# A linear-attention block with a gated FFN on one core: x's last rows written out whole in DRAM, w1's blocks paired into tiles, and the order of additions and lo parts

## The chip, the cores and the metric

The kernel runs on one core of a Trainium2 chip. The core has the engines TensorE (PE in the profile; its weight loads are the row PEld), VectorE (DVE), ScalarE (ACT), GpSimd (POOL) and SyncE (SP). SP issues all DMA transfers here, and sixteen DMA engines carry them out. Times are microseconds of device time of one execution. The kernel before took a median of 1215.95 us over three runs (1214.75 to 1216.89).

## The reference

With x of 2048 x 576 (S x D), 32 heads of 18, and F = 4608:

```
xn  = layernorm(x)
q, k, v = split(xn @ wqkv)                       # 32 heads of 18
pq, pk  = phi(q), phi(k)                         # t + 1 where t > 0, else exp(t); + 1e-6
kv, z   = sum over s of pk v', sum over s of pk
o   = (pq @ kv) / (pq . z + 1e-6)
s   = o @ wo
g   = silu(gelu(xn @ w1 + b1) @ w2 + b2)         # 576 -> 4608 -> 576
out = x + s * g
```

## The kernel before

Every float32 matrix product is made of three fp32r products: an operand is split into a hi part (a cast by ACT) and a lo part (the value less its hi part, one subtraction), and hi x hi, hi x lo and lo x hi are added in PSUM. So each operand costs a copy on ACT and a subtraction, mostly on DVE.

**Phase 1** (to about 155 us) normalises x in sixteen tiles of 128 rows (`t`), makes k and v and adds up kv and z. On the side it forms operands of w2 and stores them in DRAM.

**Phase 2** (to about 298 us) is a loop over `i` = 1 to 19: PE makes the query of tile `i` (`query`), transposes the normalised query of tile `i - 2` (`ptp`, L560) and multiplies that of tile `i - 4` with the folded kv and wo (`attend`, L569). `normalize(i)` has DVE form the sum `den`, and POOL `pbuf` (L543), which the transpose of the next-but-one iteration reads. `beside(i, k)` (L776) places other work there: with k = 0 ahead of `den`, with k = 2 ahead of `normalize`. This is the preparation of x for the FFN.

**The FFN** treats x as two halves of 1024 rows, and each half as two blocks of 512. Both of its products, x @ w1 ("Up") and h @ w2 (the down products, `pm`), use a scheme of seven products in place of eight on 2 x 2 blocks. So x is needed as seven operands (`h0`, `h1`, `s1`, `s2`, `s4` and parts of them, made by `XSums`), and w1 too. The sums sum1 to sum4 of `XSums` are DVE additions of 1024 columns, in the table `SUMS`; `SPLITS` says when each is split into hi and lo. D is 576 = 4 x 128 + 64. The 64 last rows of a block are handled on their own by `Rest`: `gather` collects them, `whole` adds hi and lo, stores them in DRAM (`rr_dram`) and loads them back shifted, `sums` forms the sums, `split` makes hi and lo of q (k = 0) and e (k = 1) and stores these in `rq_dram`. `load_rest` then fills the last column block of an operand, 128 rows of 512: four times the hi rows (one broadcast load of 32 rows), and then the lo rows over rows 32 to 63 (a second load into the same tile). The table `RESTS` says in which iteration each part runs. Half 1 of x is used first; half 0 is kept in `x_dram` and `rq_dram` and loaded at the change of halves (`load_x_part`, L1183).

The FFN runs 18 steps: nine groups of 512 columns of w1 (and rows of w2) for half 1 of x, called the first half here, and the same nine for the other half, the second half. A step has two Ups (j = 0 and 1, one `W1` object each, n = 2 step + j) and then 14 down products, and so 28 places, numbered 0 to 27 from its base: 7 for each Up, one per product in the order UP = (1, 6, 7, 5, 2, 3, 4), and 14 for the down products. After each, `at_step` emits the work that the plan has put there. DVE, ACT, POOL and PE execute exactly in the order in which this emits (`in_order`, L55); only SP's order is left to the scheduler.

In the first half a `W1` loads two raw blocks of w1 (`w1raw`), POOL forms the sums for products 5, 6, 7 and 4 in place (`T`, L627), and for each tile `hi` copies (ACT), `lo` subtracts (DVE, two instructions: L657 and, for the last rows, L659) and stores the tile in DRAM. `P1` and `P0` give the places of `T`, `hi` and `lo`. Step s takes the `W1` of its second Up through `P1` in places 0 to 4, that is during its first Up, and that of the next step's first Up through `P0`, with "a" (blocks 1 and 2 in one tile) in place 14 and the rest in 24 to 27. In the second half `W1Loaded` loads the stored tiles.

An Up (L912 to L939) has one PSUM tile each for its products; DVE adds them: u1 after product 6 (L921), u2 after 7 (L924), b after 5 (L927, in place of PSUM's B), e after 3 (L934), zy after 4 (L938), and GELU on ACT follows b, e, zy and a (after product 2). Product 3 adds on to the same PSUM bank E that L927 reads, so PE can't begin it before L927 has run. `at_step` comes behind the product's own addition. Of h, POOL forms the sums (L991 to L1000), ACT and DVE the hi and lo parts (`h_h`, `h_l`); `macc` (L1040) is DVE's addition of down products. After the change of halves `start_with_b2` loads b2 into `macc` once more.

Of the kernel before, what the change touches and what calls it, by code (L numbers as in the profile page):

```python
# [8 lines left out]
F32 = mybir.dt.float32  # L9
# [31 lines left out]
def linear_attention_gated_ffn(ctx, tc, x, wqkv, wo, w1, b1, w2, b2, out):  # L41
# [274 lines left out]
    class XSums:  # L316
# [290 lines left out]
    W1_N = {"a": 10, "b": 5, 4: 5, 5: 5, 6: 5, 7: 5}  # L607
    W1_TAG = {"a": ("wa", 2), "b": ("wb", 2)}

    def w1_tile(i, n):  # L610
        tag, bufs = W1_TAG.get(i, ("wt", 5))
        return w1p.tile([P, W1_N[i], P], F32R, tag=tag, name=f"w{i}_{n}", bufs=bufs)

    class W1:
# [3 lines left out]
        def __init__(self, n):  # L618
            self.n = n
            raw = stage_w1(f"w1raw{n}")  # L620
            nc.sync.dma_start(raw, w1[n % NP])
# [24 lines left out]
        def hi(self, i):  # L646
            self.tiles[i] = t = w1_tile(i, self.n)
            nc.scalar.copy(t[:, : 6 if i == "a" else 3], self.src[i])

        def lo(self, i):  # L650
            t, src = self.tiles[i], self.src[i]
            if i == "a":
                two = lambda v: v.rearrange("p (h k) c -> p h k c", h=2)
                hi, src, lo = two(t[:, :6]), two(src), two(t[:, 6:])
            else:
                hi, src, lo = t[:, None, :3], src[:, None], t[:, None, 3:]
            EL1.tensor_tensor(lo, src[:, :, :2], hi[:, :, :2].bitcast(F32), op=SUB)  # L657
            r = hi[64:96, :, 2]
            EL1.tensor_tensor(r, src[64:96, :, 2], r.bitcast(F32), op=SUB)  # L659
            keep_op(w1_dram, (self.n, i), t)  # L660

        def product(self, i):

            if i in (1, 2):
                t, k = self.tiles["a"], i - 1
                return t[:, 3 * k : 3 * k + 2], t[:, 6 + 2 * k : 8 + 2 * k], t[:, 3 * k + 2]
            t = self.tiles["b" if i == 3 else i]
            return t[:, :2], t[:, 3:], t[:, 2]
# [27 lines left out]
    class Rest:  # L696
# [4 lines left out]
        def tmp(self, tag, n):  # L701
            bufs, k = (2, 10) if tag == "wa" else (5, 5)
            t = w1p.tile([P, k, P], F32R, tag=tag, name=f"rest{self.half}{n}", bufs=bufs)
            return t.rearrange("p k c -> p (k c)")

        def gather(self):
            t = self.tmp("wa", "q").bitcast(F32)
            self.q, lo = t[:, :512], t[:, 512:1024]
# [6 lines left out]
        def whole(self):  # L715
# [3 lines left out]
            t = self.tmp("wa", "ef").bitcast(F32)  # L719
            self.e, self.f = t[:, :512], t[:, 512:1024]  # L720
            self.g, self.m = (self.tmp("wt", n).bitcast(F32)[:, :512] for n in "gm")
# [8 lines left out]
        def split(self, k):  # L730
            src = (self.q, self.e)[k]
            h, l = (self.tmp("wt", f"{k}{v}")[:, :512] for v in "hl")
            nc.scalar.copy(h, src)
            nc.vector.tensor_tensor(l, src, h.bitcast(F32), op=SUB)
            nc.sync.dma_start(rq_dram[self.half, k, 0], h.bitcast(F32))
            nc.sync.dma_start(rq_dram[self.half, k, 1], l.bitcast(F32))
# [31 lines left out]
    }  # L768
    SPLITS = {8: (0, 1), 9: (0, 3), 10: (0, 2), 11: (0, 4), 13: (1, 1), 14: (1, 2), 15: (1, 4)}

    RESTS = {
        3: (0, ("gather",)), 4: (0, ("whole",)), 6: (0, ("split",)), 8: (0, ("sums", "split")),
        9: (1, ("gather",)), 11: (1, ("whole",)), 13: (1, ("split",)), 15: (1, ("sums", "split")),
    }

    def beside(i, k):  # L776

        if k == 0:
# [7 lines left out]
            for half, n, j in SUMS.get(i, ()):  # L786
                getattr(xsum[half], f"sum{n}")(j)
            if i in RESTS:
                half, what = RESTS[i]
                if half not in rests:  # L790
                    rests[half] = Rest(half)
                for w in what:
                    getattr(rests[half], w)(*((int(w == "split" and "sums" in what),) if w == "split" else ()))
        else:
            if i in SPLITS:
                half, n = SPLITS[i]
                z = xsum[half]
                if i == 8:
                    z.place(True)
                if i == 13:  # L800
                    z.place(False)
# [13 lines left out]
            if i == 17:  # L815
                w, z = w1t[0], xsum[1]
                z.split(z.u, z.s3, nc.vector)
# [4 lines left out]
            if i == 18:  # L822
                w, z = w1t[0], xsum[1]
                for j in (7, 5, "b", 4):
# [226 lines left out]
    def load_xs(t):  # L1051
        F = lambda v: v.bitcast(F32)
        if t < 2:
# [113 lines left out]
    def x_operands(h0, l0, h1, l1, s1, s2, s4, rs):  # L1167
# [10 lines left out]
        "h1": (8, x_hi, 3, 7), "l1": (12, x_lo, 3, None), "s1": (20, x_lo, 0, None),  # L1178
        "s4": (24, x_lo, 1, None),
# [15 lines left out]
    def plan_w1(add, w, base, T, hi, lo):  # L1195
# [6 lines left out]
        hi={"a": 0, 6: 2, 7: 2, 5: 3, "b": 4, 4: 4},  # L1202
        lo={"a": 0, 6: 2, 7: 2, 5: 3, "b": 4, 4: 4},
# [3 lines left out]
        hi={"a": 14, 6: 25, 7: 26, 5: 26, "b": 27, 4: 27},  # L1207
        lo={"a": 14, 6: 25, 7: 26, 5: 26, "b": 27, 4: 27},
# [36 lines left out]
    add(1, start_with_b2)  # L1245
# [3 lines left out]
    for step in range(n_chunks):  # L1249
# [136 lines left out]
```

## Time and profile before

| what | value |
|---|---|
| median of three runs | 1215.95 us (1214.75 to 1216.89) |
| the profiled execution | 1213.32 us, span 1211.5 us |
| mean granted clock of TensorE | 0.973 |
| busy: PE, PEld | 1129.1 us (93%), 1035.2 us (85%) |
| busy: DVE, ACT, POOL | 863.7 us (71%), 469.9 us (39%), 462.5 us (38%) |
| DMA | 268.20 MB in 90385 packets |
| chain that ended last, by engine | PE 70%, DVE 10%, DMA 9%, issue 4%, ACT 3%, POOL 2% |

Times within the execution count from the start of the span. The windows give, for a stretch A:B, its length, then the busy time and number of instructions of each engine, the granted clock of TensorE (1.00 is full), the mean busy share of the sixteen DMA engines, and GB/s. A row of a timeline gives start, duration, engine, line, operation, out<-in; in brackets stands the time for which the engine was idle before it and what released it. A row of the chain gives start, duration, and the work that the end was waiting for.

### The profile page before, as it was taken

How to read it: one execution, taken by the hardware profiler on the slowest of the kernel's cores; microseconds unless marked ns; L12 is line 12 of the kernel's file. 1: busy time of each engine (PE TensorE's matmuls, PEld its weight loads, DVE VectorE, ACT ScalarE, POOL GpSimd, SP SyncE). 2: the span in 40 equal slices, each digit the busy share in tenths (PEclk: the TensorE clock that was granted, in tenths of full speed). 3: DMA queues.
4: the chain of work that ended last, by engine and by line, in shares of the span. 5: the costliest groups of instructions: out<-in, count | busy, mean ns of one | idle time of the engine just before them, and what ended most of it. 6: DMA issues, size and time to landing. Idle time of an engine off the chain costs nothing.

```text
span 1211.5 us, 18780 instructions
## 1 busy us (share of the span) xinstructions
PE 1129.1 (93%) x6972; PEld 1035.2 (85%) x6972; DVE 863.7 (71%) x1298; ACT 469.9 (39%) x802; POOL 462.5 (38%) x372
## 2 busy tenths in 40 slices
PE   8999999998889898988989889487999999999998
PEld 8999989998678797977879789377889889989988
DVE  6666659886788787888879888244647647656766
ACT  4444443333525344343543434231422422422432
POOL 4465533232545153452534533130423423423330
PEclk9999999998999999999999999897999999999999
DMA  7678532453894847557484658697766676676443
GB/s 273 223 286 303 204 90 81 179 216 124 285 382 153 313 158 267 212 191 279 152 308 176 227 221 273 241 323 265 275 228 213 216 234 216 213 235 210 136 149 125
DMA packets 90385, 268.20 MB, mean 221 GB/s; under 512 B 10101, under 2 KB 20597, under 8 KB 86711
## 3 DMA queue, kind: packets, MB, share of 16 engines
q1 hardware_dynamic: 90295, 267.01, 62.2%
q8 instruction: 55, 0.90, 0.3%
q14 instruction: 35, 0.29, 0.1%
HBM read 167.18 MB, written 97.85 MB: 219 GB/s over the span
## 4 chain that ended last, share of the span: by engine, by line
PE 70%; DVE 10%; DMA 9%; issue 4%; ACT 3%; POOL 2%; SPq 1%; DVEq 0%; ACTq 0%; POOLq 0%
PE pm L1031 26%; PE e L901 8%; PE zy L901 7%; PE a L901 6%; PE pv L221 5%; PE pk L221 5%; PE b L901 3%; PE pq L221 3%; DMA op<-w 2%; PE ps_s L578 2%; PE pd L1143 2%; DVE h_l L605 2%; DMA rx<-rq_dram 1%; DVE w L657 1%; PE ps_kva L258 1%
## 5 line engine op out<-in xcount | busy, mean ns | idle before, releaser
L1040 DVE TENSOR_TENSOR macc<-pm,macc 128x576 f32<-128x576 f32 x234 | 176.2, 753 | 68.7 <-PE pm L1031 53.5
L602 ACT CAST h_h<-g 128x512 fp32r<-128x512 f32 x204 | 120.9, 621 | 163.0 <-PE pm L1031 161.9
L605 DVE TENSOR_TENSOR h_l<-g,h_h 128x512 fp32r<-128x512 f32 x204 | 160.1, 791 | 0.0
L1000 POOL TENSOR_TENSOR mid<-g 128x512 f32<-128x512 f32 x34 | 44.1, 1296 | 195.0 <-ACT g L909 195.0
L909 ACT ACTIVATE g<-b,b1c 128x512 f32<-128x512 f32 x36 | 24.8, 689 | 134.2 <-DVE b L927 134.2
L635 POOL TENSOR_TENSOR w1raw<-w1raw 128x384 f32<-128x384 f32 x18 | 21.9, 1215 | 132.1 <-issue 115.4
L994 POOL TENSOR_TENSOR g<-g 128x512 f32<-128x512 f32 x34 | 52.7, 1551 | 39.7 <-DVE h_l L605 38.4
L918 ACT COPY mid<-a 128x512 f32<-128x512 f32 x36 | 21.1, 585 | 111.6 <-PE a L901 111.6
L921 DVE TENSOR_TENSOR mid<-b,mid 128x512 f32<-128x512 f32 x36 | 24.9, 691 | 54.6 <-PE b L901 43.2
L901 PE MATMUL e<-s,wb 128*128 128x512 f32 x108 | 38.0, 500 | 26.5 <-DVE b L927 26.3
L901 PE MATMUL zy<-xh,w 128*128 128x512 f32 x162 | 55.9, 398 | 2.5 <-DMA xh<-rq_dram 2.5
L1118 POOL TENSOR_TENSOR fin1l<-fin1h,fin1l 128x288 f32<-128x288 f32 x8 | 6.5, 810 | 133.4 <-PE pm L1031 58.0
L901 PE MATMUL zy<-h1r,w 128*128 128x512 f32 x162 | 55.3, 396 | 0.7 <-DVE macc L1044 0.7
L997 POOL TENSOR_TENSOR g<-g 128x512 f32<-128x512 f32 x34 | 55.0, 1617 | 2.7
L901 PEld LDWEIGHTS e<-s,wb 128*128 128x128 f32 x108 | 24.7, 238 | 36.1 <-DVE b L927 30.8
L901 PE MATMUL a<-h0r,wa 128*128 128x512 f32 x162 | 55.6, 397 | 0.0
L901 PE MATMUL a<-xh,wa 128*128 128x512 f32 x162 | 55.4, 396 | 0.0
L991 POOL TENSOR_TENSOR g<-g 128x512 f32<-128x512 f32 x34 | 46.6, 1372 | 2.7
L927 DVE TENSOR_TENSOR b<-e,mid 128x512 f32<-128x512 f32 x36 | 25.2, 699 | 30.8 <-PE e L901 30.2
L605 DVE TENSOR_TENSOR h_l<-mid,h_h 128x512 fp32r<-128x512 f32 x34 | 45.0, 1323 | 1.3
L543 POOL TENSOR_TENSOR pbuf<-phiq,den 128x576 f32<-128x576 f32 x16 | 19.4, 1212 | 68.9 <-DVE den L542 60.3
L909 ACT ACTIVATE g<-e,b1c 128x512 f32<-128x512 f32 x36 | 24.8, 690 | 51.2 <-DVE e L934 51.2
(791 smaller groups left out, 3644.3 us busy)
## 6 DMA issues: line engine op xcount, KB each, us to landing
op<-w SPq DMA_DIRECT2D x72, 320.0 KB
w<-op SPq DMA_DIRECT2D x72, 320.0 KB
op<-w2o SPq DMA_DIRECT2D x27, 576.0 KB
w1raw<-w SPq DMA_DIRECT2D x18, 768.0 KB
w2raw<-w SPq DMA_DIRECT2D x10, 1152.0 KB
op_a<-wa SPq DMA_DIRECT2D x18, 640.0 KB
wa<-op_a SPq DMA_DIRECT2D x18, 640.0 KB
w2r<-w SPq DMA_DIRECT2D x9, 1152.0 KB
```

Of the source, the lines that this page charges most:

```text
L221: nc.tensor.matmul(ps[:, h, :HD], st, w[:, k, h * HD : (h + 1) * HD], start=(i == 0), stop=(i == len(seq) - 1),)
L602: nc.scalar.copy(pair[0], src)
L605: eng.tensor_tensor(pair[1], src, pair[0].bitcast(F32), op=SUB)
L901: nc.tensor.matmul(ps, st, mv, start=first and n == 0, stop=n == len(seq) - 1, skip_group_check=True,)
L909: nc.scalar.activation(g, ps, AF.Gelu_apprx_tanh, bias=b1c[:, f : f + 1])
L927: tt(B, E, u2_sb, op=ADD)
L991: tt(src[5, pr], A(1, 0), A(1, 1), op=ADD)
L994: tt(src[6, pr], src[5, pr], A(0, 0), op=SUB)
L997: tt(src[3, pr], A(0, 1), src[6, pr], op=SUB)
L1000: tt(src[7, pr], A(0, 0), A(1, 0), op=SUB)
L1031: nc.tensor.matmul(ps[:, q, :HD], hs[p][st][:, cs], m[:, p, :], start=(n == 0 and i not in CHAIN), stop=(n == len(seq) - 1), skip_group_ch ...
L1040: nc.vector.tensor_tensor(dst, src, dst, op=ADD)
```

## The change

1. `w1_tile`, `W1`: blocks 7 and 3 go into one tile "c", blocks 5 and 4 into one tile "d", laid out as "a" is. There are four tiles (a, 6, c, d) with four copies, four pairs of subtractions and four stores, in place of six. The pools become four buffers for a, c and d and two for 6. `W1Loaded` loads four tiles.
2. `P1` and `P0`: in the first Up, lo 6 moves from place 2 to 3, c is in 4, d in 5 (hi) and 6 (lo), so that each stands behind the addition of that place. The next step's "a" moves from place 14 to 6 (hi) and 7 (lo).
3. `Rest`: `split` stores hi, lo, hi, hi into the four row groups of each product's 128 x 512 block of `rq_dram`, and `load_rest` is one load of such a block.
4. `SUMS`, `SPLITS`, `RESTS`: for half 0, the split of q in iteration 5 (was 6), the sums in 6 and the split of e in 7 (both 8). For half 1, gather in 8 (was 9), whole in 9 (11), split of q in 11 (13), sums in 13 and split of e in 14 (both 15). The sums of x's other rows are shifted; the last two splits are in 17.
5. s1 and s4 swap their buffers; two x tiles at the end of the last step take other buffers.

```diff
-    rq_dram = dram.tile([2, 2, 2, P, 512], F32, name="rq_dram")
+    rq_dram = dram.tile([2, 8, P, 512], F32, name="rq_dram")
...
-                s2, s1, s4 = self.tiles = x_hi(0, "s2"), x_lo(0, "s1"), x_lo(1, "s4")
+                s2, s1, s4 = self.tiles = x_hi(0, "s2"), x_lo(1, "s1"), x_lo(0, "s4")
...
-    W1_N = {"a": 10, "b": 5, 4: 5, 5: 5, 6: 5, 7: 5}
-    W1_TAG = {"a": ("wa", 2), "b": ("wb", 2)}
     def w1_tile(i, n):
-        tag, bufs = W1_TAG.get(i, ("wt", 5))
-        return w1p.tile([P, W1_N[i], P], F32R, tag=tag, name=f"w{i}_{n}", bufs=bufs)
+        k, tag, bufs = (5, "w6", 2) if i == 6 else (10, "wa", 4)
+        return w1p.tile([P, k, P], F32R, tag=tag, name=f"w{i}_{n}", bufs=bufs)
...
-            self.src = {"a": self.f0, "b": self.f1[:, 3:]}
+            self.src = {"a": self.f0, "c": self.f1, "d": self.f0}
...
-            nc.scalar.copy(t[:, : 6 if i == "a" else 3], self.src[i])
+            nc.scalar.copy(t[:, : 3 if i == 6 else 6], self.src[i])
...
+            key, k = {1: "a0", 2: "a1", 7: "c0", 3: "c1", 5: "d0", 4: "d1"}[i]
...
-            two = w1r.tile([P, 2, 5, P], F32R, tag="stw", name=f"w67_{n}")
-            for i in ("a", 6, 7, 5, "b", 4):
-                self.tiles[i] = t = two[:, i - 6] if i in (6, 7) else w1_tile(i, n)
+            for i in ("a", 6, "c", "d"):
+                if i == "c":
+                    t = w1r.tile([P, 10, P], F32R, tag="stw", name=f"wc_{n}")
+                else:
+                    t = w1_tile(i, n)
+                self.tiles[i] = t
                 nc.sync.dma_start(t.bitcast(F32), w1_dram[n % NP, i])
...
-            nc.sync.dma_start(rq_dram[self.half, k, 0], h.bitcast(F32))
-            nc.sync.dma_start(rq_dram[self.half, k, 1], l.bitcast(F32))
+            for n, v in enumerate((h, l, h, h)):
+                nc.sync.dma_start(
+                    rq_dram[self.half, 4 * k : 4 * k + 4, 32 * n : 32 * n + 32], v.bitcast(F32)
+                )
...
-    REST_AT = {1: (0, 0), 2: (0, 1), 4: (0, 3), 7: (1, 0), 5: (1, 1), 3: (1, 2), 6: (1, 3)}
+    REST_AT = {1: 0, 2: 1, 4: 3, 7: 4, 5: 5, 3: 6, 6: 7}
     def load_rest(half, i, dst):
-        k, at = REST_AT[i]
-        rows = slice(32 * at, 32 * at + 32)
-        dst = dst.bitcast(F32)
-        hi, lo = (rq_dram[half, k, v, rows] for v in range(2))
-        nc.sync.dma_start(
-            dst, bass.AP(tensor=hi.tensor, offset=hi.offset, ap=[[0, 4], [512, 32], [1, 512]])
-        )
-        nc.sync.dma_start(dst[32:64], lo)
+        nc.sync.dma_start(dst.bitcast(F32), rq_dram[half, REST_AT[i]])
...
     SUMS = {
-        4: ((0, 1, 0), (0, 1, 1)), 5: ((0, 1, 2), (0, 3, 0)), 6: ((0, 3, 1), (0, 3, 2)),
-        7: ((1, 1, 0), (1, 1, 1)), 8: ((0, 2, 0),), 9: ((0, 2, 1),),
-        10: ((0, 4, 0), (0, 4, 1)), 11: ((1, 1, 2),), 12: ((1, 3, 0), (1, 3, 1)),
-        13: ((1, 2, 0), (1, 2, 1)), 14: ((1, 4, 0), (1, 4, 1)), 15: ((1, 3, 2),),
+        4: ((0, 1, 0), (0, 1, 1)), 5: ((0, 1, 2), (0, 3, 0)), 6: ((0, 3, 1),),
+        7: ((0, 3, 2), (1, 1, 0)), 8: ((0, 2, 0), (1, 1, 1)), 9: ((0, 2, 1),),
+        10: ((0, 4, 0), (0, 4, 1)), 11: ((1, 1, 2),), 12: ((1, 2, 0), (1, 2, 1)),
+        13: ((1, 3, 0),), 14: ((1, 3, 1),), 15: ((1, 4, 0),), 16: ((1, 4, 1), (1, 3, 2)),
     }
-    SPLITS = {8: (0, 1), 9: (0, 3), 10: (0, 2), 11: (0, 4), 13: (1, 1), 14: (1, 2), 15: (1, 4)}
+    SPLITS = {8: (0, 1), 9: (0, 3), 10: (0, 2), 11: (0, 4), 12: (1, 1), 14: (1, 2), 17: (1, 4)}
     RESTS = {
-        3: (0, ("gather",)), 4: (0, ("whole",)), 6: (0, ("split",)), 8: (0, ("sums", "split")),
-        9: (1, ("gather",)), 11: (1, ("whole",)), 13: (1, ("split",)), 15: (1, ("sums", "split")),
+        3: (0, "gather"), 4: (0, "whole"), 5: (0, "split", 0), 6: (0, "sums"), 7: (0, "split", 1),
+        8: (1, "gather"), 9: (1, "whole"), 11: (1, "split", 0), 13: (1, "sums"), 14: (1, "split", 1),
     }
...
+            if i == 16:
+                sums(i)
+            if i == 17:
+                z = xsum[1]
+                z.split(z.u, z.s3, nc.vector)
...
     P1 = dict(
         T={5: 1, 6: 1, 7: 1, 4: 2},
-        hi={"a": 0, 6: 2, 7: 2, 5: 3, "b": 4, 4: 4},
-        lo={"a": 0, 6: 2, 7: 2, 5: 3, "b": 4, 4: 4},
+        hi={"a": 0, 6: 2, "c": 4, "d": 5},
+        lo={"a": 0, 6: 3, "c": 4, "d": 6},
     )
     P0 = dict(
         T={5: 24, 6: 24, 7: 25, 4: 25},
-        hi={"a": 14, 6: 25, 7: 26, 5: 26, "b": 27, 4: 27},
-        lo={"a": 14, 6: 25, 7: 26, 5: 26, "b": 27, 4: 27},
+        hi={"a": 6, 6: 25, "c": 26, "d": 27},
+        lo={"a": 7, 6: 25, "c": 26, "d": 27},
     )
...
-            add(base + 13, lambda n=2 * step + 2: plan_w1(add, w1t[n], base, **P0))
+            add(base + 1, lambda n=2 * step + 2, base=base: plan_w1(add, w1t[n], base, **P0))
```

More of the change, by code (lines that the diff above doesn't have):

```diff
@@ L699, in __init__, with two @@
             self.b = (xh[2 * half], xh[2 * half + 1])
[L701 to L704, printed above, removed]
+        def two(self, n):
+            t = w1_tile("a", f"rest{self.half}{n}").rearrange("p k c -> p (k c)")
+            return t[:, :512], t[:, 512:1024]
         def gather(self):
-            t = self.tmp("wa", "q").bitcast(F32)
-            self.q, lo = t[:, :512], t[:, 512:1024]
+            self.q, lo = (v.bitcast(F32) for v in self.two("q"))
             for b in range(2):
@@ L718, in whole @@
             nc.sync.dma_start(rr, q)
-            t = self.tmp("wa", "ef").bitcast(F32)
-            self.e, self.f = t[:, :512], t[:, 512:1024]
-            self.g, self.m = (self.tmp("wt", n).bitcast(F32)[:, :512] for n in "gm")
+            self.e, self.f = (v.bitcast(F32) for v in self.two("ef"))
+            self.g, self.m = (v.bitcast(F32) for v in self.two("gm"))
             A0, B0, A1, B1 = (rr[32 * k : 32 * k + 32] for k in range(4))
@@ L785, in beside @@
                 xsum[1] = XSums(2, lambda name: as2(kw_pair(name).rearrange("p a d -> p (a d)")[:, :1024]))
-            for half, n, j in SUMS.get(i, ()):
-                getattr(xsum[half], f"sum{n}")(j)
+            sums(i)
             if i in RESTS:
-                half, what = RESTS[i]
+                half, what, *k = RESTS[i]
                 if half not in rests:
                     rests[half] = Rest(half)
-                for w in what:
-                    getattr(rests[half], w)(*((int(w == "split" and "sums" in what),) if w == "split" else ()))
-        else:
+                getattr(rests[half], what)(*k)
+        else:
+            if i == 16:
+                sums(i)
+            if i == 17:
+                z = xsum[1]
+                z.split(z.u, z.s3, nc.vector)
             if i in SPLITS:
@@ L797, in beside @@
                 z = xsum[half]
[L798 to L801, printed above, removed]
+                if i in (8, 12):
+                    z.place(not half)
                 z.split(z.u if n == 3 else z.t, getattr(z, f"s{n}"), nc.vector)
@@ L815, in beside @@
             if i == 17:
-                w, z = w1t[0], xsum[1]
-                z.split(z.u, z.s3, nc.vector)
+                w = w1t[0]
                 w.hi("a"), w.lo("a")
@@ L822, in beside @@
             if i == 18:
-                w, z = w1t[0], xsum[1]
-                for j in (7, 5, "b", 4):
+                w = w1t[0]
+                for j in ("c", "d"):
                     w.hi(j), w.lo(j)
```

32 lines of the change are left out of this document (17 added, 15 removed).

## The prediction

> **What bounds the kernel now.** I read the page first, then the busy time by windows, then the chain that ended last, and at each place where the chain leaves TensorE (PE) the engines' timelines. The page gives the span. The windows give the busy us of PE, weight loads, DVE, ACT and POOL, then the clock, the DMA share and GB/s. The last rows are the chain's, at the first product of a step.
>
> ```profile
> span 1211.5 us, 18780 instructions
> ```
> ```profile
> 450.00:500.00 50.00, 45.67 (x258) 40.48 (x257) 41.94 (x65) 21.64 (x39) 22.90 (x17) 0.97 0.61 222
> 950.00:1000.00 50.00, 50.00 (x289) 44.91 (x288) 32.55 (x44) 17.11 (x29) 17.76 (x14) 1.00 0.69 226
> ```
> ```profile
> 404.30 1.64 PE a L901 x7
> 455.74 1.64 PE a L901 x7
> 842.99 1.62 PE a L901 x7
> 887.98 1.62 PE a L901 x7
> ```
>
> PE never rests in the second half; in the first it waits or runs at half clock. A step takes 51.4 us in the first half (455.74 - 404.30) and 45.0 in the second (887.98 - 842.99), though PE does the same products. Five steps on from 455.74, step 8 starts near 713; step 10 starts at 842.99. Steps 8 and 9 thus take 130 us against 90.
>
> Where the 6.4 us of a first-half step go is seen in the chain, in the timelines of DVE and PE, and in a window:
>
> ```profile
> 464.41 1.51 DVE w L657
> ...
> 466.25 0.71 DVE b L927
> ```
> ```profile
> 459.45 0.42 DVE L659 TENSOR_TENSOR wa<-w1raw,wa 32x256 fp32r<-32x256 f32 x1
> 462.70 0.67 DVE L657 TENSOR_TENSOR w<-w1t,w 128x256 fp32r<-128x256 f32 x1 [1.31 <-ACT w L648]
> 463.39 0.99 DVE L659 TENSOR_TENSOR w<-w1t,w 32x128 fp32r<-32x128 f32 x1
> 480.45 1.63 DVE L605 TENSOR_TENSOR h_l<-mid,h_h 128x512 fp32r<-128x512 f32 x1
> ```
> ```profile
> 467.00 2.76 PE L901 MATMUL e<-s,wb 128*128 128x512 f32 x6 [3.25 <-DVE b L927]
> 483.12 0.43 PE L1031 MATMUL pm<-w__5132,h_h 128*128 128x288 f32 x2
> 489.32 0.53 PE L1031 MATMUL pm<-w__5158,h_h 128*128 128x288 f32 x2 [1.08 <-DVE macc L1040]
> ```
> ```profile
> 467.20:470.60 3.40, 3.40 (x9) 2.65 (x9) 2.35 (x6) 3.40 (x7) 0.00 (x0) 0.50 0.49 193
> ```
>
> The addition b (L927) needs only product 5, which is over at 462.13 (row below). But on DVE it stands behind the lo parts of tiles 6 and 7, which wait for ACT's copies and, through them, for POOL's sums. PE waits 3.25 us, then has half clock for 3.4 us (1.7 lost). It waits 1.08 us more for a macc sum that stands behind the lo part of the next step's "a". That is 6.03 of the 6.4.
>
> **The change, part by part.** *The steps.* With blocks 7 and 3 in tile c and 5 and 4 in tile d, six copies, twelve subtractions and six stores per W1 become four, eight and four, of the same elements and bytes; SP has 72 issues fewer, and is no bound here. In the changed order DVE runs u1, u2, b, lo 6, w2's lo, lo c, w2's lo, e, w2's lo, zy, lo d, and then the next a. Durations, from the same step:
>
> ```profile
> 461.74 0.39 PE L901 MATMUL e<-rx,w 128*128 128x512 f32 x1
> 460.70 0.69 DVE L924 TENSOR_TENSOR mid<-zy,mid 128x512 f32<-128x512 f32 x1
> 458.75 0.69 DVE L657 TENSOR_TENSOR wa<-w1raw,wa 128x512 fp32r<-128x512 f32 x1 [0.23 <-ACT wa L648]
> 468.88 0.76 DVE L605 TENSOR_TENSOR w__5132<-w2raw,w__5132 128x576 fp32r<-128x576 f32 x1
> 457.88 0.84 ACT L648 CAST wa<-w1raw 128x768 fp32r<-128x768 f32 x1
> 467.97 0.67 ACT L602 CAST w__5132<-w2raw 128x576 fp32r<-128x576 f32 x1
> 468.55 0.69 ACT L909 ACTIVATE g<-a,b1c 128x512 f32<-128x512 f32 x1
> 464.20 1.44 POOL L954 TENSOR_TENSOR w2raw<-w2raw 128x576 f32<-128x576 f32 x1
> ```
>
> I lay the order out by hand from 462.13, each operation after the one before it on its engine and after what it reads. b runs from 462.15 to 462.85. Product 2 covers it, so the 3.25 us and the half clock go. What is late next is tile d for the second Up.
> ACT: GELU b, w2's copy, GELU a, c's copy (0.84), w2's copy, to 466.1.
> DVE: lo 6 to 464.6 (0.67 and 0.99, what it takes now beside POOL), w2's lo 465.4, lo c 466.6 (0.69 and 0.42), w2's lo 467.3, e 468.0.
> ACT: GELU e, d's copy, the third w2 copy, to 470.1. DVE: its lo 470.8, zy 471.5, lo d 472.65. PE gets to product 5 of the second Up at 471.65 and waits 1.0.
> ACT: GELU zy, the next a's copy (moved from step 14 to 6), m1's copy, to 473.5. DVE: lo a 474.1, u1, u2, b to 476.3. PE waits 0.6 before product 3.
> Then come h's lo parts, at 0.7 to 1.63 us by whether POOL works. That of (1,1) ends near 480.9; the down products, begun at 479.5 instead of 483.12, want it five matmuls later, at 480.2: 0.7.
> New waits are 2.3. The late macc goes, as lo a has left that place. A step gains 6.03 - 2.3 = 3.7; eight steps (1 to 8), less the 1.08 that step 8 has no next W1 for, gain 28.8. Ends for the new waits: 1.0 (d's alone) and 6.0 (all that goes comes back).
>
> The moved copy of a holds ACT's queue, with m1's copy, the GELUs and all h behind it, until w1raw has landed:
>
> ```profile
> 460.35 0.50 SPq L621 DMA_DIRECT2D w1raw<-w  x1
> ```
> ```profile
> 468.00:469.00 1.00, 1.00 (x4) 0.81 (x3) 0.83 (x3) 1.00 (x3) 0.00 (x0) 0.50 0.02 5
> ```
>
> It is issued at 460.35, and at 468 the DMA engines are empty (share 0.02), so it has landed by then, 4 us before ACT gets to the copy at 472.1. As many bytes are issued ahead of it as before. Cost 0; without that cover each us late costs a us in each of eight steps. The second w1raw now waits on SP for lo d; behind it stand only stores that nobody soon waits for: 0.
>
> *Phase 2 and step 0.*
>
> ```profile
> 284.11 1.33 PE L560 MATMUL ptp<-ident,pbuf 128*128 128x128 f32 x5 [3.78 <-POOL pbuf L543]
> 224.41 0.53 PE L578 MATMUL ps_s<-kw_h,th 128*128 128x288 f32 x2 [1.62 <-ACT s L583]
> 305.54 0.47 PE L901 MATMUL zy<-xh,w 128*128 128x512 f32 x1 [2.48 <-DMA xh<-rq_dram]
> ```
> ```profile
> 277.83 0.74 DVE L740 SCALAR_TENSOR_TENSOR rest1ef<-rest1ef,sgn 128x512 f32<-128x512 f32 x1
> 280.76 0.69 DVE L734 TENSOR_TENSOR rest11l<-rest1ef,rest11h 128x512 fp32r<-128x512 f32 x1 [0.68 <-ACT rest11h L733]
> ```
> ```profile
> 282.90:289.70 6.80, 5.59 (x24) 5.59 (x25) 4.07 (x7) 3.15 (x5) 1.22 (x2) 0.50 0.40 132
> ```
>
> In iteration 15 the last rows' sums and split (277.83 to 281.45, 3.6 us) and one x split stand ahead of den, on which pbuf waits. They go to iterations 13, 14 and 17. den then ends near 278.0 and pbuf at 279.2, before PE asks for it at 280.3. The 3.78 us go, and half of the 6.8 at half clock, 3.4. The 1.62 us at 224.41 come from the same sums in iteration 8, now in 6: 1.6. DVE gets no more work in all. Half 1's rows are added up one iteration after their gather instead of two, as half 0's are today; a wait there is bounded by the 1.6. Step 0 waits 2.48 us for product 7's rows and then loses 1.7 to the clock: on SP each load of lo rows waits until the broadcast load that it overwrites has landed. One transfer a product needs no such wait; four stores write what two did, twice the bytes, while the DMA share is 0.40. The sum is 8.8 + 4.2 - 2.3 (step 0's own new waits) = 10.7. Ends: 2 and 14.
>
> *The change of halves.* The chain, PE's timeline and three windows:
>
> ```profile
> 770.09 9.39 DMA rx<-rq_dram
> 779.50 8.47 DMA rx<-rq_dram
> ```
> ```profile
> 788.11 0.76 PE L901 MATMUL e<-rx,w 128*128 128x512 f32 x1 [12.15 <-DMA rx<-rq_dram]
> ```
> ```profile
> 744.00:748.00 4.00, 4.00 (x32) 4.00 (x31) 4.00 (x5) 1.27 (x3) 3.58 (x3) 1.00 0.36 118
> 766.00:770.00 4.00, 0.47 (x1) 0.19 (x1) 1.37 (x3) 3.13 (x3) 0.00 (x0) 1.00 0.42 135
> 776.00:790.00 14.00, 1.89 (x5) 1.53 (x6) 0.70 (x1) 0.35 (x1) 0.00 (x0) 0.69 0.32 102
> ```
>
> Of the 40 us that steps 8 and 9 lose, 5 are step 8's own wait and clock; 35 belong here. x, w1, w2 and the rows all come through DMA, which is far from full in three windows, where SP waits for broadcast loads. Their empty part is 4 x 0.64 + 4 x 0.58 + 14 x 0.68 = 14.4 us. I take 14: the later transfers, b2's for macc among them, move up by this and no more, as the bytes stay. Ends: 0, if SP's other waits fill the windows, and 24, if PE's half clock there goes too.
>
> Phase 1 and the second half keep their order, and the swap of s1 and s4 and the new places of the last x tiles follow buffers that are free earlier: 0.
>
> **The sum.** 28.8 + 10.7 + 14 = 53.5. The profiled execution took 1213.3 us, of which 1211.5 are span, so 1160. The median of the runs shown, 1215.95, is 2.6 above it.
>
> **The rivals.**
> (a) POOL holds DVE. At 464.41 a subtraction of 256 columns took 1.51 us beside POOL. If the first w2 lo part cannot start before POOL's sum ends (464.20 + 1.44), it ends at 466.4 and lo d 0.9 later: 9 x 0.9 = 8, so 1168. Against it: L924, which reads PSUM, took its 0.69 beside POOL. The Trainium skill's page "SBUF — State Buffer" (SBUF: two separate sides) has DVE operations with two SBUF inputs and GpSimd's exclude each other for whole instructions; the two rows agree.
> (b) The stall moves: ACT's copies and the three w2 lo parts delay the second Up by as much as the first was. The steps then give 0 and phase 2 and the halves stay: 1213.3 - 10.7 - 14 = 1189. For it: DVE is 84% busy there (41.94 of 50). Against it: the layout above.
> (c) The single transfers change nothing at the change of halves, since bytes bound it: 1174. Against it: the share of 0.32.
> (d) Slower: w1raw lands late, and ACT stands at a's copy. With 53.5 to lose in eight steps, this decides at 6.7 us behind 472.1: w1raw would land after 478.8, 18 us after its issue. At 7.5 late the time is 1220. For it: SP's order is new around it. Against it: the empty queue at 468.
>
> **How the numbers follow.** Forecast 0.55, (a) 0.15, (b) 0.11, (c) 0.09, (d) 0.10. Low end: new waits of 1.0 (1.3 x 9 = 12) and 24 at the change of halves (10 more), 1138. High end: (b) with 4 at the change of halves, 1199, so 1200. A difference of 0.2% (2.4 us) is about what can be told from none. All but (d) are faster, 0.88; 0.02 is for a (d) that balances, 0.10 for slower.
>
> **What would show it.** Right: first-half steps near 47.7 us, b directly behind product 5, no half clock in that half, waits near 1 us at product 5 of the second Up; no wait for pbuf in iteration 15; no load from rq_dram in the chain at the change of halves. Wrong: ACT waiting for w1raw's DMA at step 6, or an addition in the second Up for which PE waits 3 us.

## The result and the profile after

The changed kernel takes 1179.74 us (median of 4 runs, 1176.41 to 1180.71), the kernel before 1215.97 beside it (4 runs): a ratio of 0.9698, with an interval of 0.9677 to 0.9719. The profiled executions took 1213.32 and 1179.50: 33.8 us gained where the forecast's sum had 53.5. The sums below are made against these two.

The page of the changed kernel, and its windows (columns as in the prediction: PE, weight loads, DVE, ACT, POOL, clock, DMA share, GB/s):

```profile
span 1177.7 us, 18497 instructions
```
```profile
450.00:500.00 50.00, 46.17 (x259) 40.50 (x258) 41.89 (x58) 21.94 (x36) 22.87 (x17) 0.97 0.60 223
750.00:800.00 50.00, 42.78 (x236) 38.16 (x236) 28.24 (x38) 19.29 (x28) 15.26 (x10) 0.93 1.02 351
950.00:1000.00 50.00, 50.00 (x289) 44.88 (x288) 29.80 (x41) 16.63 (x27) 16.05 (x14) 1.00 0.69 216
```

The first row is nearly what it was: PE 46.17 instead of 45.67, the clock still 0.97, DVE still 42 of 50. The chain that ended last has the starts of steps 1, 2, 3, 9 and 10:

```profile
351.15 1.62 PE a L901 x7
401.99 1.62 PE a L901 x7
452.86 1.62 PE a L901 x7
...
754.25 1.62 PE a L901 x7
...
808.46 1.62 PE a L901 x7
```

A first-half step takes 50.87 us, not 47.7. Step 9 takes 54.2, where it took 80.7 (762.1, read in PE's timeline, to 842.83). PE's timeline shows what waits are left:

```profile
320.63 0.79 PE L901 MATMUL a<-xh,wa 128*128 128x512 f32 x1 [10.14 <-ACT mid L918]
...
419.08 1.20 PE L901 MATMUL e<-s,wd 128*128 128x512 f32 x4 [0.61 <-DVE wd L657]
424.99 2.72 PE L901 MATMUL e<-s,wc 128*128 128x512 f32 x6 [2.70 <-DVE b L927]
...
786.33 0.53 PE L1031 MATMUL pm<-w__7712,h_h 128*128 128x288 f32 x2 [1.47 <-DVE macc L1040]
793.92 0.82 PE L1031 MATMUL pm<-w__7751,h_h 128*128 128x288 f32 x2 [5.75 <-issue]
```

The wait for b is back, at product 3 of the second Up instead of the first. And there is one new, long wait in step 0 (the first row). The last two rows, in step 9, are waits while b2 is loaded into `macc`; a run below takes most of them away. This is DVE in step 2, and POOL beside it:

```profile
418.34 0.68 DVE L657 TENSOR_TENSOR wd<-w1raw,wd 128x512 fp32r<-128x512 f32 x1
...
419.91 1.27 DVE L657 TENSOR_TENSOR wa<-w1raw,wa 128x512 fp32r<-128x512 f32 x1 [0.44 <-ACT wa L649]
421.20 1.42 DVE L659 TENSOR_TENSOR wa<-w1raw,wa 32x256 fp32r<-32x256 f32 x1
422.64 0.69 DVE L921 TENSOR_TENSOR mid<-b,mid 128x512 f32<-128x512 f32 x1
423.44 0.69 DVE L924 TENSOR_TENSOR mid<-zy,mid 128x512 f32<-128x512 f32 x1
424.24 0.70 DVE L927 TENSOR_TENSOR b<-e,mid 128x512 f32<-128x512 f32 x1
```
```profile
419.23 1.40 POOL L1000 TENSOR_TENSOR mid<-g 128x512 f32<-128x512 f32 x1 [7.29 <-ACT g L909]
420.71 1.62 POOL L991 TENSOR_TENSOR g<-g 128x512 f32<-128x512 f32 x1
```

The lo part of the next a (place 7) stands ahead of u1, u2 and b. It takes 2.7 us, with POOL's first two sums for h beside it; that these are the reason is tested below. In step 0 it is ACT that stands, at the copy for the next a:

```profile
319.26 0.83 ACT L649 CAST wa<-w1raw 128x768 fp32r<-128x768 f32 x1 [10.12 <-DMA op<-w__3588]
```
```profile
296.45 2.41 SPq L867 DMA_DIRECT2D macc<-b  x2
298.96 0.61 SPq L600 DMA_DIRECT2D op_a<-wa  x1
299.67 2.46 SPq L621 DMA_DIRECT2D w1raw<-w  x1
```

The release is put down to a store; what the copy reads is w1raw, issued at 299.67, behind the two loads of b2 (296.45).

Where the time went, by stage (each stage from the first product of a step to the next, in us, from PE's timelines):

| kernel | phases 1, 2 | step 0 | steps 1 to 8 | step 9 | rest |
|---|---|---|---|---|---|
| before | 298.4 | 54.3 | 409.4 | 80.7 | 368.7 |
| after | 291.5 | 59.5 | 403.1 | 54.2 | 369.4 |
| forecast gain | 8.8 | 1.9 | 28.8 | 14 | 0 |
| measured gain | 6.9 | -5.2 | 6.3 | 26.5 | -0.7 |

So the total hides errors of both signs.

### The profile page after: what moved, and what is told of

Its sections match the earlier page's. It is cut to its first block, busy times and chain, and to the rows that moved or that the text cites. A ratio compares the mean times of both kernels' runs of the same rounds, so it can differ in the third digit from the quotient of the medians.

```text
span 1177.7 us, 18497 instructions
## 1 busy us (share of the span) xinstructions
PE 1123.4 (95%) x6972; PEld 1028.9 (87%) x6972; DVE 852.0 (72%) x1226; ACT 465.7 (40%) x766; POOL 461.7 (39%) x372
## 4 chain that ended last, share of the span: by engine, by line
PE 79%; DVE 10%; issue 5%; DMA 3%; ACT 2%; POOL 0%; DVEq 0%; ACTq 0%; POOLq 0%
PE pm L1031 30%; PE e L901 8%; PE zy L901 7%; PE a L901 6%; PE pk L222 5%; PE pv L222 5%; PE ps_s L579 5%; PE pq L222 4%; PE b L901 4%; PE pd L1143 2%; DMA op<-w__3588 1%; PE ps_kva L259 1%; DVE h_l L606 1%; DMA kr<-kw 1%; DVE macc L1040 1%
## 5 line engine op out<-in xcount | busy, mean ns | idle before, releaser
L606 DVE TENSOR_TENSOR h_l<-g,h_h 128x512 fp32r<-128x512 f32 x204 | 157.4, 779 | 0.0
L901 PE MATMUL e<-s,wc 128*128 128x512 f32 x108 | 34.8, 467 | 19.2 <-DVE b L927 19.2
L901 PEld LDWEIGHTS a<-xh,wa 128*128 128x128 f32 x162 | 30.9, 191 | 19.4 <-ACT mid L918 13.0
L901 PEld LDWEIGHTS e<-s,wc 128*128 128x128 f32 x108 | 22.9, 219 | 27.8 <-DVE b L927 22.9
L934 DVE TENSOR_TENSOR e<-e,mid 128x512 f32<-128x512 f32 x36 | 25.0, 693 | 23.7 <-PE e L901 23.6
L291 POOL TENSOR_TENSOR w2r<-w2r 128x576 f32<-128x576 f32 x27 | 41.8, 1553 | 0.7
```

Source lines behind the costliest of these rows:

```text
L606: eng.tensor_tensor(pair[1], src, pair[0].bitcast(F32), op=SUB)
L901: nc.tensor.matmul(ps, st, mv, start=first and n == 0, stop=n == len(seq) - 1, skip_group_check=True,)
```

## The experiments

All were timed beside the kernel before, on the same chip within a group; ratios are to it. The kernel before took 1213.70 to 1216.81 us in the four groups, so a difference of up to 3 us between groups says nothing.

**What holds the steps.** Theory: the order on DVE, made worse by POOL. Rival: DVE has no room at all.

```diff
-        lo={"a": 7, 6: 25, "c": 26, "d": 27},
+        lo={"a": 24, 6: 25, "c": 26, "d": 27},
```

> The changed kernel, with the lo part of the next step's tile a moved from place 7 to place 24, and nothing else. Theory T (order on DVE): in the second Up of steps 1 to 7 this part, two subtractions of 1.27 and 1.42 us beside POOL's sums, stands ahead of u1, u2 and b, and is what product 3 waits for (2.69 us and then 3.41 us at half clock). Without it u1 can begin when ACT's copy of m1 ends (471.24), b ends near 474.0, and PE waits 0.8 instead of 2.7, at full clock: 1.9 + 1.7 = 3.6 a step, 25 in seven steps, so 1155; up to 8 more, 1163, if DVE has no room at place 24 and a macc sum comes late again. Rival R (DVE is full, 42 of 50.9 us, and the wait turns up elsewhere): steps stay near 50.9 and the time at 1174 to 1180.

At place 24 POOL's sum for block 5 has already written over part of the source, so the values of this lo part aren't those of a; the instructions are the same. Measured: 1155.39 (ratio 0.9495, 0.9481 to 0.9509). Steps 1 to 7 take 47.3, as the theory had it; b's wait is 0.44 and the half clock is gone:

```profile
417.81 1.65 PE L901 MATMUL e<-s,wc 128*128 128x512 f32 x6 [0.44 <-DVE b L927]
422.41 0.40 PE L1031 MATMUL pm<-w__4552,h_l 128*128 128x288 f32 x1 [0.45 <-DVE h_l L606]
```

```diff
-        hi={"a": 6, 6: 25, "c": 26, "d": 27},
-        lo={"a": 7, 6: 25, "c": 26, "d": 27},
+        hi={"a": 14, 6: 25, "c": 26, "d": 27},
+        lo={"a": 14, 6: 25, "c": 26, "d": 27},
```

> The changed kernel, with the copy and the lo part of the next a at place 14, as before. Theory T (order of DVE and ACT): b ends near 473.2 in the second Up, PE waits about 0.1 and keeps full clock (4.3 a step gained), but a macc sum comes 1.08 late again: 3.2 a step, 22 in seven steps; in step 0 ACT no longer stands at place 6, 7 to 12 more. 1146 to 1151. Rival R (DVE full): steps stay at 50.9 and only step 0 gains, 1168 to 1173.

Measured: 1153.66 (0.9476, 0.9461 to 0.9491), a little above the forecast of 1146 to 1151. Steps take 48.0, a gain of 2.9 where 3.2 was forecast. At place 14 the lo part is again beside POOL's sums, and a macc sum is late, by the amount that it was late before the change:

```profile
369.52 0.40 PE L1031 MATMUL pm<-w__4073,h_l 128*128 128x288 f32 x1 [0.45 <-DVE h_l L606]
374.99 0.54 PE L1031 MATMUL pm<-w__4093,h_h 128*128 128x288 f32 x2 [1.08 <-DVE macc L1040]
```

So with this one piece of the change undone the kernel is 26 us faster than the whole change: 20.3 of it in steps 1 to 8, 8.5 in step 0 (59.5 to 51.0), less 2.2 in phases 1 and 2. Whether POOL is part of the cause is asked by leaving its two sums out:

```diff
+            skip = pr == 0 and 0 < self.c < NC - 1 and self.first_half
             if i == 5:
...
-                tt(src[5, pr], A(1, 0), A(1, 1), op=ADD)
+                skip or tt(src[5, pr], A(1, 0), A(1, 1), op=ADD)
...
-                tt(src[7, pr], A(0, 0), A(1, 0), op=SUB)
+                skip or tt(src[7, pr], A(0, 0), A(1, 0), op=SUB)
```

> The changed kernel without POOL's first two sums for h's first pair (operands 7 and 5) in steps 1 to 7, the two that run while DVE makes the next a's lo part in the second Up; the sums are left out, the copies and products that read them stay. Theory T (DVE is slowed by POOL's sums beside it): that lo part takes 0.69 and 0.42 us as it does where POOL is idle, 1.58 less than 1.27 and 1.42, so PE's wait for b falls from 2.69 to about 1.1 and half clock goes: 2.5 to 3.3 a step, 1157 to 1162. Rival R (the part is slow for another reason, such as its own address or the copy before it): b's wait stays near 2.7 and the time at 1178 to 1181.

Measured: 1163.58 (0.9572, 0.9549 to 0.9594), just above the theory's 1157 to 1162 and far from the rival; its profiled execution took 1159.3. The part takes 0.69 and 0.42, and PE's wait is 2.69 - 1.58 = 1.1:

```profile
366.54 0.69 DVE L657 TENSOR_TENSOR wa<-w1raw,wa 128x512 fp32r<-128x512 f32 x1 [0.44 <-ACT wa L649]
367.24 0.42 DVE L659 TENSOR_TENSOR wa<-w1raw,wa 32x256 fp32r<-32x256 f32 x1
```
```profile
370.04 1.66 PE L901 MATMUL e<-s,wc 128*128 128x512 f32 x6 [1.10 <-DVE b L927]
```

POOL's presence is shown to cost these 1.58 us. The Trainium skill's page "SBUF — State Buffer" (SBUF: two separate sides) says that a DVE operation with two SBUF inputs and a GpSimd operation that reads SBUF exclude each other; by that rule the trace agrees, though it shows the subtractions as longer and not as later.

The order alone, in the kernel before:

```diff
-        lo={"a": 0, 6: 2, 7: 2, 5: 3, "b": 4, 4: 4},
+        lo={"a": 0, 6: 3, 7: 3, 5: 4, "b": 4, 4: 5},
```

> The kernel before, with one line changed: in the first Up the lo parts of W1's tiles 6 and 7 come at place 3 (behind b), 5 at place 4 and 4 at place 5. Nothing else of the change. Theory T (order on DVE): product 3 of the first Up no longer waits 3.25 us nor runs 3.4 us at half clock; tile 5 or 4 is late by about 1 instead: 4 a step in nine steps, 36, so about 1180. Rival R (DVE has no room, the wait moves to the second Up): 0 to 1 a step, 1207 to 1216.

Measured: 1193.96 (0.9818, 0.98 to 0.9836), between the two forecasts. Steps take 48.4 instead of 51.4: 23.6 in steps 1 to 8, of which step 0 loses 2.6 again (57.0). The 3.25 us and the half clock go, but three smaller waits of 0.4 to 0.5 us come, of which these are two, and the late macc sum stays:

```profile
421.11 0.50 PE L901 MATMUL a<-xh,wa 128*128 128x512 f32 x1 [0.48 <-ACT mid L918]
423.43 1.63 PE L901 MATMUL e<-s,wb 128*128 128x512 f32 x6 [0.45 <-DVE b L927]
...
433.52 0.53 PE L1031 MATMUL pm<-w__4651,h_h 128*128 128x288 f32 x2 [1.10 <-DVE macc L1040]
```

**Step 0.** Theory: w1raw is queued behind b2.

```diff
-    add(0, start_with_b2)
+    add(1, start_with_b2)
```

> The changed kernel, with the loads of b2 into macc back at place 1 of step 0, behind the issue of w1raw. Theory T: in step 0 ACT stands 10 us at the copy for the next a because w1raw is queued behind b2's 2.3 MB; with w1raw ahead the stand shrinks to the 2.7 us of the other steps, and half clock from 13.65 to 3.41 us: 7.4 + 5.1 = 12.5, so 1167, or up to 4 more (1171) if a macc sum then waits for b2. Rival R: w1raw is late for another reason (its own buffer, or the DMA engines full with stores), and the time stays at 1178 to 1181.

Measured: 1169.66 (0.9611, 0.9595 to 0.9627). Step 0 takes 51.2 instead of 59.5. SP now issues w1raw at 293.32, ahead of b2, and PE waits 2.68 for b, as in the other steps:

```profile
293.32 0.80 SPq L621 DMA_DIRECT2D w1raw<-w  x1
294.43 0.57 SPq L600 DMA_DIRECT2D op_a<-wa  x1
295.09 2.38 SPq L867 DMA_DIRECT2D macc<-b  x2
```

**The single transfers.** Four runs: two loads in the changed kernel, the single load alone in the kernel before, the broadcast without the second load, and four plain loads.

```diff
-        nc.sync.dma_start(dst.bitcast(F32), rq_dram[half, REST_AT[i]])
+        src, dst = rq_dram[half, REST_AT[i]], dst.bitcast(F32)
+        nc.sync.dma_start(
+            dst, bass.AP(tensor=src.tensor, offset=src.offset, ap=[[0, 4], [512, 32], [1, 512]])
+        )
+        nc.sync.dma_start(dst[32:64], src[32:64])
```

> The changed kernel, with each product's last rows loaded in two transfers again (32 rows broadcast to 128, then the lo rows over them), from the same expanded rows in DRAM. Theory T (the prediction): the single transfer is what empties SP's waits, worth 14 at the change of halves and about 4 in step 0: 1194 to 1198. Rival R (the gain at the change of halves came from tiles that are free earlier, so that x and W1 are issued within step 8): 1180 to 1184.

Measured: 1225.74 (1.0071, 1.0056 to 1.0086), 46 us slower than the changed kernel. That is more than either forecast. Step 9 takes 83.3, as before the change, and step 0 takes 80.8: PE waits there for three products' rows, and 13.38 for the next a's copy, since w1raw is issued behind all these loads.

```diff
+            for n, v in enumerate((h, l, h, h)):
+                nc.sync.dma_start(
+                    rq_dram[self.half, 4 * k : 4 * k + 4, 32 * n : 32 * n + 32], v.bitcast(F32)
+                )
...
+        nc.sync.dma_start(dst.bitcast(F32), rq_dram[half, 4 * k + at])
```

> The kernel before, with the last rows expanded in DRAM by four stores and loaded by one transfer a product; tiles, order and sums as before. Theory T (the single transfer alone moves step 9): step 9 falls from 80.7 to about 54 and step 0 loses its wait of 2.5 and the half clock behind it: 27 + 4, so 1185 to 1189. Rival R (it also needs the four buffers of tiles a, c and d, by which x and W1 are issued earlier): step 9 falls by the 14 of the prediction or less, 1198 to 1204.

Measured: 1190.37 (0.9801, 0.9785 to 0.9817), just above the theory's range. Step 9 falls from 80.7 to 57.0 by this part alone (the theory had about 54). Step 0 doesn't gain (53.9): PE waits 5.69 there for rows, as it does (5.68) in the run with the old sums below, so with late sums and four stores the rows come late. The late sums alone don't do it: the run with four plain loads below has the same sums, but two stores, and no such wait. In this run SP waits for the last store of the rows to land before it can go on (SP's waits from 280 to 312: us in total, times, longest):

```profile
SPq L752 <- DMA rq_dram<-rest11h: 7.5, 1, 7.5
```

The loads for which PE waits are issued behind that, at 305.15. The prediction's "twice the bytes, while the DMA share is 0.40" put the two added stores at nothing; in the changed kernel the sums are early enough to cover them. The stores weren't tested by themselves.

The changed kernel with the broadcast load in place of the plain one:

```diff
-        nc.sync.dma_start(dst.bitcast(F32), rq_dram[half, REST_AT[i]])
+        src = rq_dram[half, REST_AT[i]]
+        nc.sync.dma_start(
+            dst.bitcast(F32), bass.AP(tensor=src.tensor, offset=src.offset, ap=[[0, 4], [512, 32], [1, 512]])
+        )
```

> The changed kernel, with each product's last rows loaded in one transfer, but of the 32 hi rows broadcast to four groups (the lo rows are not loaded, hi rows stand in their place). It separates the two things that the change removes: the broadcast's slow transfer and the wait of the lo rows' load for it. Theory T (both count: in the kernel before, four broadcast loads held the chain for 9.39 us and the four loads of lo rows behind them for 8.47): about half of what the two loads cost comes back, step 9 at 62 to 70 and the time between 1192 and 1210. Rival R1 (only the wait counts): as the changed kernel, 1178 to 1182. Rival R2 (only the rate of the broadcast counts): as with two loads, 1220 to 1226.

Measured: 1207.37 (0.9947, 0.9926 to 0.9967), within the theory's range for the time, but step 9 takes 74.6, above its 62 to 70, and step 0 takes 67.7. Of the 29.1 us that step 9 loses between one load and two (83.3 - 54.2), the second load and its wait are 8.7, and the broadcast's own slowness 20.4.

```diff
-        nc.sync.dma_start(
-            dst, bass.AP(tensor=hi.tensor, offset=hi.offset, ap=[[0, 4], [512, 32], [1, 512]])
-        )
-        nc.sync.dma_start(dst[32:64], lo)
+        for n, v in enumerate((hi, lo, hi, hi)):
+            nc.sync.dma_start(dst[32 * n : 32 * n + 32], v)
```

> The kernel before, with each product's last rows loaded by four transfers of 32 rows (hi, lo, hi, hi), which write different partitions and need not wait for one another; DRAM holds the rows once, as before. Theory T (the broadcast's form is slow, not reading the same rows four times): step 9 falls as with the single transfer, to 57 to 61, and the time to 1190 to 1195. Rival R (rows must lie apart in DRAM to be read fast, as b2's did in e8_reordered_b2_rows): step 9 stays near 80 and the time near 1212 to 1216.

Measured: 1197.65 (0.9867, 0.9843 to 0.9891), between the two forecasts. Step 9 takes 66.6, 14.1 less than before, and step 0 takes 51.4, 2.9 less. So the form of the broadcast is slow, and the same rows, read four times, are much less so; what is left against the single load (9.6 us) may be the 28 issues in place of seven or the reading, and wasn't separated. The prediction's row of 776 to 790 has a DMA share of 0.32 and 102 GB/s, the changed kernel's loads of the same rows run in a full window:

```profile
743.00:749.00 6.00, 6.00 (x47) 6.00 (x46) 5.67 (x9) 2.37 (x4) 0.00 (x0) 1.00 1.03 422
```

The Trainium skill's page "DMA: Bandwidth & Descriptors" (Why a DMA increments its semaphore by 16 and not by 1) says that a copy is spread over the largest number of engines, 16 at most, that divides the slowest dimension of both sides. The broadcast's source has 4 as its slowest dimension, so by that page it would use 4 of 16, an estimated share of 0.25; the trace agrees (a share of 0.32, with loads of 32 rows in the same window).

**The sums of phase 2.** The tables SUMS, SPLITS and RESTS as in the kernel before, all else as changed:

```diff
-        3: (0, "gather"), 4: (0, "whole"), 5: (0, "split", 0), 6: (0, "sums"), 7: (0, "split", 1),
-        8: (1, "gather"), 9: (1, "whole"), 11: (1, "split", 0), 13: (1, "sums"), 14: (1, "split", 1),
+        3: (0, "gather"), 4: (0, "whole"), 6: (0, "split", 0), 8: (0, "sums"),
+        9: (1, "gather"), 11: (1, "whole"), 13: (1, "split", 0), 15: (1, "sums"),
...
```

> The changed kernel, with the sums of x, its splits and the last rows' sums back in the iterations of phase 2 in which the kernel before has them; tiles, transfers and the steps stay. Theory T (the prediction): the last rows' sums stand ahead of den again, PE waits 1.6 in iteration 8 and 3.8 in iteration 15 and then has half clock: 7 to 9 lost against the changed kernel, so 1187 to 1189, and up to 4 more if the rows then land late in step 0 (1193). Rival R (other places cost nothing, since single transfers and four buffers already free DVE's waits): 1179 to 1181.

Measured: 1189.48 (0.9781, 0.9763 to 0.9798): 9.7 lost against the changed kernel. Phases 1 and 2 end 7.2 later, by the two waits of the kernel before, and step 0 takes 61.6:

```profile
284.38 1.33 PE L561 MATMUL ptp<-ident,pbuf 128*128 128x128 f32 x5 [3.81 <-POOL pbuf L544]
```

**A faster version.** Tile d a place earlier, the next a where DVE and ACT have room, b2 behind w1raw:

```diff
-        hi={"a": 0, 6: 2, "c": 4, "d": 5},
-        lo={"a": 0, 6: 3, "c": 4, "d": 6},
+        hi={"a": 0, 6: 2, "c": 4, "d": 4},
+        lo={"a": 0, 6: 3, "c": 4, "d": 5},
...
-        hi={"a": 6, 6: 25, "c": 26, "d": 27},
-        lo={"a": 7, 6: 25, "c": 26, "d": 27},
+        hi={"a": 14, 6: 25, "c": 26, "d": 27},
+        lo={"a": 22, 6: 25, "c": 26, "d": 27},
...
-    add(0, start_with_b2)
+    add(1, start_with_b2)
```

> The changed kernel with three edits: the next a's copy at place 14 and its lo part at place 22 (before POOL overwrites its source at 24), tile d's copy at place 4 and its lo part at 5, b2's loads at place 1 of step 0. Theory T (order on DVE): no wait for b, none for d, no late macc sum: steps of 48.0 (with a at 14) less 1.07 and 0.62, 46.3; step 1 begins near 337, step 9 near 707, and with 55 for step 9 and 371 behind it the time is 1133. Rival R (DVE is full): at place 22 the lo part makes macc sums late by about a microsecond again and d's wait turns up at another product: 1142 to 1148.

Measured: 1140.97 (0.938, 0.9362 to 0.9399). Steps take 46.2, without half clock, as the theory had it. DVE is busy there for 44.8 of 50 us (450 to 500) and PE for 49.3, so DVE had room, and the rival is out for the steps. The profiled execution's 1138.8 is 5.8 above the forecast: step 9 takes 59.2 instead of 55, step 0 49.1 instead of 47 (PE waits 2.16 there for an operand of w2).

The next edit adds the change's own idea for b2: one transfer in iteration 3 writes it to DRAM 512 times over.

```diff
+    b2x_dram = dram.tile([P, QH, D], F32, name="b2x_dram")
...
+                nc.sync.dma_start(
+                    b2x_dram, bass.AP(tensor=b2.tensor, offset=b2.offset, ap=[[0, P], [0, QH], [1, D]])
+                )
...
-                bass.AP(tensor=b2.tensor, offset=b2.offset, ap=[[0, P], [0, QH], [1, D]]),
+                b2x_dram,
```

> The kernel of the run e7_reordered, and b2 expanded in DRAM once in phase 2 (one transfer from DRAM to DRAM), so that macc is loaded from rows of its own in steps 0 and 9 instead of from one row read 512 times. Theory T (the price of a broadcast load is the one source, not the bytes): in step 9 b2 no longer moves at 150 GB/s for 13 us; the waits for macc there (4.1 to 4.4 and 3.2 to 3.9 us) and their half clock go, 8 to 11: 1122 to 1125. Rival R (bytes and DMA engines bound step 9, which stays at 55): 1133, or slower if the transfer in phase 2 delays x's loads.

Measured: 1127.55 (0.9274, 0.9256 to 0.9291), the fastest of all, though 2.6 above the forecast's range. Step 9 takes 49.8, and PE's two waits there fall from 4.64 and 4.45 to 1.56 and 1.16. While most of b2 was loaded, the changed kernel's DMA engines were full at 177 GB/s (780 to 790); here they are full at 404. The first row is the changed kernel's, the second this one's:

```profile
780.00:790.00 10.00, 6.71 (x49) 6.24 (x47) 4.37 (x6) 3.37 (x6) 4.20 (x3) 1.00 1.03 177
```
```profile
735.00:750.00 15.00, 12.27 (x91) 11.84 (x90) 9.69 (x14) 4.57 (x8) 5.50 (x4) 1.00 1.03 404
```

## Why the prediction was right and where it was wrong

It said faster, and the time lies in its range, but three of its four terms were badly sized. That the total still fell into the range is partly luck: the steps and step 0 brought 29.6 us less than forecast, the change of halves 12.5 more.

*The steps (28.8 forecast, 6.3 measured).* The first Up went as laid out: b stands directly behind product 5, and its wait and half clock are gone. The step that failed is the layout's line "lo a 474.1, u1, u2, b to 476.3. PE waits 0.6 before product 3". I priced lo a at 0.69 and 0.42, from the lo part of the second Up's a, in a row in which POOL was idle. I had named POOL for h's lo parts, but not for this one. It takes 2.69 beside POOL. The price stood in the trace of before: at its old place the same part of the next a took 2.59, beside the same two sums of POOL:

```profile
485.88 1.17 DVE L657 TENSOR_TENSOR wa<-w1raw,wa 128x512 fp32r<-128x512 f32 x1
487.06 1.42 DVE L659 TENSOR_TENSOR wa<-w1raw,wa 32x256 fp32r<-32x256 f32 x1
```

So the move hardly changed its length, but what waits behind it: a macc sum that was 1.08 late before, u1, u2 and b now. The run without POOL's sums gives these 1.58 back, and with lo a at 24 the step takes 47.3, near the 47.7 forecast. The new waits were 3.3 (2.69 and 0.62, the latter forecast as 1.0) and half clock, not 2.3. Step 8, which has no next a to make, gained 3.3 of its own (49.9 to 46.6).

*Rival (b), the stall moves to the second Up,* is what happened in the steps, down to the addition in the second Up that PE waits 2.7 us for. I had given it 0.11, and another cause (ACT's copies and w2's lo parts). Rival (a) had the cause, POOL against DVE, but at a place, w2's lo part in the first Up, behind which PE hardly waits.

*Step 0 (1.9 forecast, 5.2 lost).* The wait for rows is gone, as forecast. Rival (d), ACT standing at a's copy, came true in this one step. "As many bytes are issued ahead of it as before" was read off a middle step. In step 0 the change also moves b2's loads from place 1 to 0, ahead of w1raw; that line stands in the whole diff, but neither in the list of the change above nor in the prediction, and so had no price. It is worth 10 us (1179.74 to 1169.66).

*Phase 2 (8.8 forecast, 6.9 measured).* Right: neither wait is there, and putting the sums back costs 7.2 there.

*The change of halves (14 forecast, 26.5 measured).* The sign and place were right: no load of rows is left in the chain. The step that failed is that the later transfers "move up by this and no more, as the bytes stay", with 14.4 us counted in three windows. SP waited for broadcast loads for longer than these show, and the chain of before has a third load of rows, ahead of the two in the prediction (first what SP waited for from 740 to 800: us in total, times, longest; then the chain's row):

```profile
SPq L755 <- DMA rx<-rq_dram: 10.8, 4, 3.6
SPq L755 <- DMA h1r<-rq_dram: 10.2, 1, 10.2
SPq L755 <- DMA h0r<-rq_dram: 8.2, 1, 8.2
```
```profile
756.74 12.03 DMA h1r<-rq_dram
```

SP's waits make 29.2 us; in the changed kernel SP waits 0.3 at most for a load of rows there. DMA was also not full earlier in step 8. The windows of 720 to 750, before and after:

```profile
720.00:750.00 30.00, 26.75 (x143) 23.26 (x141) 24.59 (x36) 15.09 (x27) 13.99 (x10) 0.94 0.66 224
```
```profile
720.00:750.00 30.00, 28.93 (x183) 26.28 (x182) 25.80 (x37) 15.95 (x26) 11.78 (x8) 1.00 1.01 405
```

There 10.2 us were empty (30 x 0.34), 2.6 of them in my 744 to 748. With 14.4 that makes 22, near the 23.7 that the single load gave alone (80.7 to 57.0), by which rival (c), bytes as the bound, is out. Putting two loads back into the changed kernel costs 29.1 there, so the loads are the cause; how the other parts share in the last 3 us wasn't separated.

*The chances.* They are added up wrongly in one place: all but (d) make 0.90, not 0.88.

## What to carry to other kernels

When work is moved to another place in an engine's queue, price it from a row in which the other engines do what they do at the new place, and ask what waits behind it there: here a part that takes 2.6 us beside POOL at either place was priced at 1.1, from a row without POOL, and came to stand in front of an addition that PE waits for. Undoing the move gave 20.3 us in steps 1 to 8. Look at the first pass of a loop by itself, since what is queued there once (here b2) can stand ahead of what every pass needs. A transfer that reads few rows many times can leave the DMA engines empty or keep them full without moving much; a copy in DRAM that is laid out as it is read took 23.7 us off one step, and another for b2 took 9.4 off the same step of the faster version (59.2 to 49.8).

## What was not expected of the hardware

Loads of one row to all partitions: most of b2's ran with the DMA engines full at 177 GB/s, where the copy with rows of its own ran at 404. In the two microseconds ahead (778 to 780) the changed kernel still moved 395 GB/s, and in the kernel before b2's load ended at 156 GB/s with a DMA share of only 0.48 (815 to 821). So full engines alone don't explain its rate; what limits it stays open.

Half clock doesn't depend on a wait's length alone. In the run with the old sums the wait for b is the same in steps 1 and 2, and only the second is followed by half clock (two rows of PE's timeline, and the windows behind them):

```profile
383.54 1.65 PE L901 MATMUL e<-s,wc 128*128 128x512 f32 x6 [2.68 <-DVE b L927]
...
433.62 1.65 PE L901 MATMUL e<-s,wc 128*128 128x512 f32 x3 [2.67 <-DVE b L927]
```
```profile
383.60:387.00 3.40, 3.40 (x16) 2.80 (x16) 3.33 (x5) 2.33 (x4) 2.71 (x2) 1.00 1.00 415
433.60:437.00 3.40, 3.38 (x8) 2.74 (x9) 2.77 (x3) 2.40 (x4) 2.63 (x2) 0.50 1.00 414
```

The step without it took 50.1 us, those with it 50.9, so a stretch of half clock costs 0.8 us here and not 1.7, in part because without it PE meets a wait of 0.45 us for a lo part of h. In the clock's records the stretches at half speed last 3.413 us or a multiple (but for the last, which the end cuts off), and begin multiples of 3.413 apart; the first wait lies across two such intervals (1.57 and 1.11 us), the second within one.

All fourteen profiles can be sorted by this grid, from 15 us after the start to 60 us before the end, by how long PE had no matmul in an interval. Of 4335 intervals at full clock, the 102 that half clock followed had 1.84 us or more, and the other 4233 had 1.89 or less. Of 168 at half clock, it went on behind the 66 with 0.64 us or more, and ended behind the 102 with 0.59 or less. So the idle time within one interval of the grid seems to decide, at about 1.85 us; this is read off the runs, and none moved a wait to test it.
